# Attention and expert layer in one kernel: rows kept unnormalised, normalised after the gather, with queue and set-up in another order

## The chip, the cores and the metric

The kernel runs on one core of a Trainium2 chip. The core has a matrix engine (TensorE, PE; its weight loads are shown apart as PEld), a vector engine (VectorE, DVE), an activation engine (ScalarE, ACT), a general engine (GpSimd, POOL) and a queue that issues most DMAs (SyncE, SP). The metric is the device time of one launch in microseconds. Before the change it is 534.06 us, the median of 3 runs (533.18 to 534.73). One more execution was profiled: it took 532.09 us, with a span of 530.4 us.

## The reference

Causal attention over 4 batches of 12 heads with 448 positions and 64 columns a head, then one of 8 experts for each of the 1792 rows, all in float32.

```python
scores = np.where(causal, -1e9, (q @ k.T) / 8);  scores -= scores.max(-1)
attn = np.exp(scores);  attn /= attn.sum(-1) + 1e-9
x = (attn @ v).transpose(0, 2, 1, 3).reshape(1792, 768)
logits = x @ w_gate + modality_bias[modality_id]
e_idx = argmax(logits);  gate_w = softmax(logits)[e_idx]
for e in range(8):
    out[e_idx == e] = gate_w * (relu(x[e_idx == e] @ w1[e]) @ w2[e])     # 768 -> 1024 -> 768
```

## The kernel before, in words

**Precision.** Every large matmul is done in parts: an operand is split into a rounded high part and the rest (hi and lo), by a copy and a subtraction, and two or three products are added up in PSUM. The copies and subtractions are the main work of POOL and DVE.

**Attention.** The 48 heads are taken one per iteration, n = 0 to 47, as a software pipeline: iteration n computes the scores of head n (PE, L277), the row max of head n with the causal mask (DVE, L284), the exponentials of head n-1 (ACT, L294, which also gives the sums), the transposes of head n-2 (PE, L306) with their split (ACT L324, DVE L325), and the product with V of head n-3 (PE, L338, then ACT L363 and DVE L369). Four heads are a group (GH=4), three groups a batch. POOL splits q and k for two heads at a time (L185, L186, L189; tiles hl and kz), and SP stacks the parts by DMAs (L197, L198, tile st). POOL also splits V of a group into vh (L252, at n = 4k) and vl (L257, at n = 4k+1); PE's L338 needs both. `load_v` on SP brings the next group's V at n = 4k+2.

**Combining and normalising.** From n = 8 on, one block of 128 rows (64 for the first of a batch, four blocks a batch) of a finished group is combined per iteration: PE multiplies by a matrix wi that holds an identity and the gate weights, so that for each of the four heads 64 values of x and its 8 parts of the logits come out (L398, 288 columns). The softmax sums of the group have been inverted by then (L376, L383, tile rec). Even blocks are normalised by DVE from PSUM (`norm_l` L416, `norm_x` L426). Odd blocks are moved by ACT to SBUF (L408, tile cxt) and normalised by POOL with the same two lines. `norm_l` writes into ltp, where every head has a slot and one more slot holds the modality bias (POOL, L392, at the start of a batch; there are two such buffers). Finished rows of 768 columns are stored to xs in DRAM.

**Routing.** After each batch its logits are summed (L458), and one-hot marks (oh, L473), places by a matmul (L480) and gates (ent, L505) are computed by small operations, spread over the next iterations. POOL scatters the row numbers into four tables in DRAM (L509). After batch 1 the first expert is chosen and its weights loaded; `pre_ids` fetches slot numbers from the tables (idq, SP, L734) and `fetch_x` gathers rows (xg, POOL, L746) for the first expert block, so that its work begins between the last heads.

**The tail and the experts.** The section "tail" holds the last heads, the first expert products (`pre_g1`) and the last batch's routing, written out by hand. Then come steps, with counts that are known only at run time: each gathers 128 or 64 rows per place, transposes them (L755), multiplies by w1 (L765 to L767), applies relu, multiplies by w2 and scatters to out. At an expert's end w1 and w2 are replaced and split anew, by all of ACT, DVE (L685) and POOL (L681, L682).

**Order.** Instructions run in the order of the program on each engine; there is no scheduler. `iteration(n)` gives the order, with lists of later work: `later(n, f)` runs f behind the scores of iteration n, `soon` and `before` at other points. In set-up, ten small DVE operations make constants (L959 to L961 at n=0, L964 to L970 at n=1).

## Time and profile before

| | |
|---|---|
| median of 3 runs | 534.06 us (533.18 to 534.73) |
| profiled execution, its span | 532.09 us, 530.4 us |
| PE, PEld busy | 481.1 us (91%), 449.5 us (85%) |
| DVE, ACT, POOL busy | 319.2 us (60%), 273.7 us (52%), 290.5 us (55%) |
| granted PE clock, mean | 0.969 |
| largest groups | L294 on ACT 94.7 us, L765 to L767 on PE 68.0 us each, L325 on DVE 58.4 us, L189 on POOL 51.5 us |

The busy shares are means over two stages that differ: attention up to about 230 us, where every engine works, and the expert steps after it, where PE works nearly alone. A time is therefore read from the stretch that it belongs to. Positions in the text are microseconds from the start of the span. PE's clock is given as a share of its full 2.4 GHz.

### The profile page before, as it was taken

What the parts mean: (1) busy time and instruction counts of PE and PEld (TensorE: products, weight loads), DVE (VectorE), ACT (ScalarE), POOL (GpSimd) and SP (SyncE); (2) the same over time, 40 slices, a digit from 0 to 9 for tenths busy, and PEclk for the clock granted to TensorE, in tenths of its full rate; (3) what the DMA queues carried; (4) which work ended last, traced back from release to release, by engine and by line L of the source; (5) the groups of instructions that cost most, each with busy time, mean ns of one, the idle gap of its engine ahead of it and who ended that gap; (6) DMA issues with size and microseconds to landing.
All of it is one profiled execution on the core that took longest, in us unless ns stands there. A gap on an engine that the chain in (4) does not pass through costs nothing. (4 is left out here: it accounts for less than half of the span.)

```text
span 530.4 us, 10338 instructions
## 1 busy us (share of the span) xinstructions
PE 481.1 (91%) x3331; PEld 449.5 (85%) x3331; DVE 319.2 (60%) x882; ACT 273.7 (52%) x683; POOL 290.5 (55%) x303
## 2 busy tenths in 40 slices
PE   4598999999988979989899999999999999989971
PEld 4488889989968878878899999999999999978751
DVE  7988889999988979897521114552011110393690
ACT  4498899999977948724321124342111211551820
POOL 7799999989798797973220201752001001193581
PEclk9799999999989979999899999999999999999986
DMA  8687789987976398656369300973101001077000
GB/s 216 169 202 191 197 219 272 265 203 193 253 209 169 112 238 254 239 164 90 90 191 376 93 31 3 318 247 92 61 1 51 30 17 76 15 254 268 4 11 6
DMA packets 44137, 80.75 MB, mean 152 GB/s; under 512 B 15646, under 2 KB 27166, under 8 KB 44064
## 3 DMA queue, kind: packets, MB, share of 16 engines
q1 hardware_dynamic: 41024, 68.89, 46.2%
q0 software_dynamic: 3040, 11.03, 6.3%
q8 instruction: 28, 0.46, 0.4%
q14 instruction: 45, 0.37, 0.2%
HBM read 49.01 MB, written 11.89 MB: 115 GB/s over the span
## 5 line engine op out<-in xcount | busy, mean ns | idle before, releaser
L294 ACT ACTIVATE p<-p,nm 128x448 f32<-128x448 f32 x192 | 94.7, 497 | 9.5 <-DVE nm L284 9.5
L746 POOL DMA_INDIRECT xg<-xs,idg x18 | 20.3, 1126 | 139.1 <-DVEq L1327 75.2
L784 DVE SCALAR_TENSOR_TENSOR htl<-g,hth 128x256 fp32r<-128x256 f32 x40 | 16.7, 423 | 108.4 <-ACT hth L783 108.4
L765 PE MATMUL g<-xh,w1h 128*128 128x256 f32 x240 | 68.0, 283 | 0.0
L767 PE MATMUL g<-xh,w1l 128*128 128x256 f32 x240 | 67.9, 283 | 0.0
L766 PE MATMUL g<-xl,w1h 128*128 128x256 f32 x240 | 67.9, 283 | 0.0
L325 DVE TENSOR_TENSOR pl<-pt,ph 128x1024 fp32r<-128x1024 f32 x48 | 58.4, 1216 | 11.1 <-ACT ph L324 10.2
L306 PE MATMUL pt<-ident,p 128*128 128x128 f32 x432 | 64.8, 278 | 0.0
L338 PE MATMUL ot<-ph,vhl 128*128 128x448 f32 x192 | 50.8, 305 | 10.5 <-POOL vhl L257 6.4
L324 ACT ACTIVATE ph<-pt 128x1024 fp32r<-128x1024 f32 x48 | 48.9, 1019 | 13.1 <-PE pt L306 12.7
L189 POOL TENSOR_TENSOR kz<-raw,hl 64x448 fp32r<-64x448 f32 x44 | 51.5, 1170 | 6.9 <-DMA table<-ent,si 4.7
L306 PEld LDWEIGHTS pt<-ident,p 128*128 128x128 f32 x432 | 53.6, 150 | 0.6 <-issue 0.2
L783 ACT ACTIVATE hth<-g 128x256 fp32r<-128x256 f32 x40 | 15.2, 382 | 65.2 <-PE g L767 65.2
L277 PE MATMUL sa<-st 128*128 128x448 f32 x96 | 32.8, 342 | 17.2 <-DVE st L229 6.6
L825 POOL DMA_INDIRECT out_dram<-row,idg x14 | 15.0, 1074 | 56.9 <-ACTq L1311 32.2
L765 PEld LDWEIGHTS g<-xh,w1h 128*128 128x128 f32 x240 | 46.0, 192 | 0.2 <-DVE htl L784 0.2
L766 PEld LDWEIGHTS g<-xl,w1h 128*128 128x128 f32 x240 | 46.0, 192 | 0.0
L767 PEld LDWEIGHTS g<-xh,w1l 128*128 128x128 f32 x240 | 46.0, 192 | 0.0
L338 PEld LDWEIGHTS ot<-ph,vhl 128*128 128x128 f32 x192 | 33.8, 195 | 13.4 <-POOL vhl L257 7.4
L284 DVE CUSTOM_DVE_ANT_0 p<-sa,mask 128x448 f32<-128x448 f32 x96 | 36.3, 413 | 4.5 <-PE sa L277 3.8
L284 DVE CUSTOM_DVE_ANT_0 p<-sb,mask 128x192 f32<-128x192 f32 x96 | 36.3, 412 | 0.2
L294 ACT ACTIVATION_READ_ACCUMULATOR p<-p,nm 128x1 f32 x192 | 36.4, 189 | 0.0
(337 smaller groups left out, 1394.1 us busy)
## 6 DMA issues: line engine op xcount, KB each, us to landing
st<-hl SPq DMA_DIRECT2D x88, 224.0 KB
raw<-in_moe_w_dram SPq DMA_DIRECT2D x24, 512.0 KB
raw<-in_qk_dram SPq DMA_DIRECT2D x22, 448.0 KB
raw<-in_moe_w_dram SPq DMA_DIRECT2D x20, 384.0 KB
vraw<-in_v_dram SPq DMA_DIRECT2D x12, 384.0 KB
xs<-row SPq DMA_DIRECT2D x12, 384.0 KB
ut<-in_moe_w_dram SPq DMA_DIRECT2D x6, 384.0 KB
raw<-in_qk_dram SPq DMA_DIRECT2D x8, 224.0 KB
```

The costliest lines, as they stand in the source:

```text
L189: P.tensor_tensor(out=kz[m % 2][r, a], in0=x[r, 1], in1=hl[r, 2].bitcast(F32), op=ALU.subtract)
L277: nc.tensor.matmul(outs[i], lhsT=a[:, q0:q0 + n], rhs=z[:, :w], start=(last == 0), stop=(last == 1))
L284: V.tensor_tensor_reduce(out=z, in0=o, in1=m, scale=-scale, scalar=3.0e38, op0=ALU.add, op1=ALU.min, accum_out=nm[:n, i:i + 1],)
L294: A.activation(out=z, in_=z, func=AF.Exp, bias=nm[:n, i:i + 1], scale=-1.0, accum_out=sums[:n, b, i, h:h + 1],)
L306: nc.tensor.transpose(out=o, in_=a, identity=ident)
L324: A.activation(out=ph, in_=t, func=AF.Copy)
L325: V.tensor_tensor(out=pl, in0=t, in1=ph.bitcast(F32), op=ALU.subtract)
L338: nc.tensor.matmul(o[:, q0:S], lhsT=t[:rows, kt, h].rearrange("p a d -> p (a d)"), rhs=ph[:rows, c0:c1], start=(n == 0), stop=(n == 1),)
L746: P.indirect_dma_start(out=xg[u][:n], out_offset=None, in_=xs[0:rows, :], in_offset=bass.IndirectOffsetOnAxis(ap=g[:n, 0:1], axis=0), boun ...
L765: nc.tensor.matmul(o, lhsT=ah, rhs=bh, start=first, stop=False)
L766: nc.tensor.matmul(o, lhsT=ah, rhs=bl, start=False, stop=False)
L767: nc.tensor.matmul(o, lhsT=al, rhs=bh, start=False, stop=last)
```

## The change

1. **Combining.** All 288 columns of a block go into the row as they are: even blocks by one DVE copy from PSUM, odd ones by ACT (`take_x`). The row gets 12 more columns for reciprocal sums, so rows, xs and gathers have 876 columns. The order of columns in a row is now pairs of heads, 128 of x and 16 of logits.
2. **Sums.** One sum operation (POOL; DVE for the last batch) and four reciprocals per batch instead of three of each.
3. **Logits.** `norm_l` works from SBUF, once per block and batch, for all 12 heads (96 columns, DVE). For the last batch the first 8 heads are done before its gate work and the last 4 from PSUM.
4. **Gathered rows** are normalised in place by `norm_g`: the first block by DVE, every other by POOL, at the start of the step before (`norm_gs`).
5. **Bias.** One ltp buffer instead of two; the bias is added at the last group of the batch.
6. **POOL and SP order.** vh and vl are both made at n = 4k+1, behind the q/k split; `load_v` is issued at n = 4k, behind the stacking; the first expert's slot numbers are fetched two iterations later, rows of the first block two and one.
7. **Set-up.** The ten constants are made at n = 4 to 8; two of three subtractions for heads 2 and 3 move from n = 1 to n = 2, behind the max.

Numbers of lines are two to thirteen higher in the changed kernel (L284 becomes L286, L505 becomes L510).

**DVE at the start.** Before: the rows between the max of head 1 and the max of head 2; L964 to L970 are constants, L232 and L229 subtractions for heads 2 and 3.

```order
L232 TENSOR_TENSOR kz_150<-raw_113,st 64x448
L229 TENSOR_TENSOR st<-raw_114,st 64x448
L232 TENSOR_TENSOR kz_150<-raw_114,st 64x448
L964 TENSOR_SCALAR eq_98<-row 128x32
L965 CAST gt_99<-row 128x32
L966 SCALAR_TENSOR_TENSOR gt_99<-row,gt_99 128x32
L967 TENSOR_SCALAR ctri<-row 128x64
L968 TENSOR_SCALAR e_80<-evals 128x32
L969 TENSOR_SCALAR ebase<-evals 128x8
L970 TENSOR_SCALAR ebneg<-ebase 128x8
L284 ISA p_3_162,nm<-sa,mask 128x448
```

And the changed kernel, from the same place to the max of head 3:

```order
L234 TENSOR_TENSOR kz_147<-raw_113,st 64x448
L286 ISA p_3_159,nm<-sa,mask 128x448
L286 ISA p_0_156,nm<-sa,mask 64x64
L286 ISA p_1_157,nm<-sb,mask 128x192
L286 ISA p_2_158,nm<-sb,mask 128x320
L231 TENSOR_TENSOR st<-raw_114,st 64x448
L234 TENSOR_TENSOR kz_147<-raw_114,st 64x448
L327 TENSOR_TENSOR pl<-pt,ph 128x1024
L286 ISA p_3_151,nm<-sa,mask 128x448
```

The constants have left this place, and two subtractions stand behind the max of head 2 instead of ahead of it.

**SP around the slot numbers.** Before: idq are the slot numbers that are read from the tables, st the stacked parts of q and k for heads 42 and 43.

```order
L179 DMA raw<-in_qk_dram 128x896
L245 DMA vraw<-in_v_dram 128x3x256
L246 DMA vraw<-in_v_dram 64x256
L734 DMA idq<-table_70 128x2
L734 DMA idq<-table_71 128x2
L734 DMA idq<-table_72 128x2
L734 DMA idq<-table_73 128x2
L197 DMA st<-hl 64x896
L198 DMA st<-hl 64x2x448
```

And the changed kernel:

```order
L199 DMA st<-hl 64x896
L200 DMA st<-hl 64x2x448
L247 DMA vraw<-in_v_dram 128x3x256
L248 DMA vraw<-in_v_dram 64x256
L678 DMA raw_112<-in_moe_w_dram 128x1024
L181 DMA raw<-in_qk_dram 128x896
L738 DMA idq<-table_70 128x2
L738 DMA idq<-table_71 128x2
```

The stacking and the load of V now stand ahead of the fetches, and the next stacking behind them is that of heads 44 and 45.

**POOL at the end of attention.** Before: L392 is the bias add of the last batch, L509 the scatters to the tables, of which the first four belong to the batch before.

```order
L392 TENSOR_SCALAR ltp<-mb 128x4x8
L746 DMA xg_124<-xs,idg_1_118 128x768
...
L509 DMA table_70<-ent,si 14592x2
L509 DMA table_71<-ent,si 14592x2
L509 DMA table_72<-ent,si 14592x2
L509 DMA table_73<-ent,si 14592x2
L1224 TENSOR_TENSOR mask<-ident 128x64
L509 DMA table_70<-ent,si 14592x2
```

And the changed kernel, where L401 is the bias add and L438 the norm of a gathered block:

```order
L438 TENSOR_TENSOR xg_124<-xg_124 128x6x128
L686 TENSOR_SCALAR w1h_3171<-raw_114 128x1024
...
L514 DMA table_70<-ent,si 14592x2
L514 DMA table_71<-ent,si 14592x2
L514 DMA table_72<-ent,si 14592x2
L514 DMA table_73<-ent,si 14592x2
L1243 TENSOR_TENSOR mask<-ident 128x64
L401 TENSOR_SCALAR ltp<-mb 128x4x8
L514 DMA table_70<-ent,si 14592x2
```

The bias add, which the logits of the last batch wait for (L463 on DVE), moved behind four scatters and the mask.

```diff
+    XR = H * XW + H
...
-    lts = [ltp[:, j] for j in range(2)]
+    ltp = cst("ltp", [128, 512])
+    lt = ltp[:, 0:NTL * (H + 1) * E].rearrange("p (t h e) -> p t h e", t=NTL, h=H + 1)
...
-    def st_sums(gr, eng):
-        b, u = divmod(gr, NG)
-        r = sm([128, NTL, GH, 1], "rec")
-        eng.tensor_scalar(
-            out=r.rearrange("p t h o -> p t (h o)"), in0=sums[:, b, :, u * GH:(u + 1) * GH],
-            scalar1=1.0, scalar2=1e-9, op0=ALU.mult, op1=ALU.add,
-        )
-        rec[gr] = r
-
-    def st_rec(gr):
-        V.reciprocal(out=rec[gr], in_=rec[gr])
+    def pairs(x, lo, hi):
+        return x.rearrange("p (j c) -> p j c", c=2 * XW)[:, :, lo:hi].rearrange("p j (a d) -> p j a d", a=2)
+
+    def xcols(x):
+        return pairs(x[:, 0:H * XW], 0, 2 * D)
+
+    def lcols(x):
+        return pairs(x, 2 * D, 2 * XW)
+
+    def recs(x):
+        return x[:, H * XW:XR].rearrange("p (j a o) -> p j a o", a=2, o=1)
+
+    def st_sums(b, eng):
+        t = sums[:, b].rearrange("p t h -> p (t h)")
+        eng.tensor_scalar(out=t, in0=t, scalar1=1.0, scalar2=1e-9, op0=ALU.mult, op1=ALU.add)
+
+    def st_rec(b):
+        for i in range(NTL):
+            V.reciprocal(out=xrow[b, i][:, H * XW:XR], in_=sums[:, b, i])
 
     def st_comb(gr, i, x=None):
         b, u = divmod(gr, NG)
         q0, n = QT[i]
         if u == 0:
             xrow[b, i] = row()
-            if i == 0:
-                lt_all[b] = lts[b % 2]
-                P.tensor_scalar(
-                    out=lts[b % 2][:, :, H, :], in0=mb[:, b], scalar1=1.0, scalar2=0.0, op0=ALU.mult, op1=ALU.add
-                )
+        if u == NG - 1 and i == 0:
+            P.tensor_scalar(out=lt[:, :, H, :], in0=mb[:, b], scalar1=1.0, scalar2=0.0, op0=ALU.mult, op1=ALU.add)
         if x is None:
             x = bank("x")
         for j in range(GH // 2):
             nc.tensor.matmul(
                 x[:n, j * 2 * XW:(j + 1) * 2 * XW], lhsT=ots(gr, j)[:, q0:q0 + n],
-                rhs=wi[:, u * (GH // 2) + j].rearrange("p a c -> p (a c)"), start=True, stop=True,
+                rhs=wi[:, u * (GH // 2) + j], start=True, stop=True,
             )
-        cx[gr, i] = V, x
-
-    def st_move(gr, i):
+        cx[gr, i] = x
+
+    def take_x(gr, i):
+        b, u = divmod(gr, NG)
+        n = QT[i][1]
+        w = GH * XW
+        o, c = xrow[b, i][:n, u * w:(u + 1) * w], cx.pop((gr, i))[:n, 0:w]
         if i % 2:
-            c = cxt[:, (i // 2) * 384:(i // 2) * 384 + GH * XW]
-            n = QT[i][1]
-            A.activation(out=c[:n], in_=cx[gr, i][1][:n, :GH * XW], func=AF.Copy)
-            cx[gr, i] = P, c
-
-    def norm_l(gr, i):
+            A.activation(out=o, in_=c, func=AF.Copy)
+        else:
+            V.tensor_copy(o, c)
+
+    def norm_l(b, i, h0, h1, x=None):
+        n = QT[i][1]
+        c = xrow[b, i][:n, h0 * XW:h1 * XW] if x is None else x[:n, 0:GH * XW]
+        j = slice(h0 // 2, h1 // 2)
+        V.tensor_tensor(
+            out=lt[:n, i, h0:h1, :].rearrange("p (j a) e -> p j a e", a=2), in0=lcols(c),
+            in1=recs(xrow[b, i])[:n, j].to_broadcast([n, (h1 - h0) // 2, 2, E]), op=ALU.mult,
+        )
+
+    def st_norm(gr, i):
+        take_x(gr, i)
         b, u = divmod(gr, NG)
-        q0, n = QT[i]
-        eng, c = cx[gr, i]
-        xv = c[:n, :GH * XW].rearrange("p (h c) -> p h c", h=GH)
-        eng.tensor_tensor(
-            out=lt_all[b][:n, i, u * GH:(u + 1) * GH, :], in0=xv[:, :, D:XW],
-            in1=rec[gr][:n, i].to_broadcast([n, GH, E]), op=ALU.mult,
-        )
-
-    def norm_x(gr, i):
-        b, u = divmod(gr, NG)
-        q0, n = QT[i]
-        eng, c = cx.pop((gr, i))
-        xv = c[:n, :GH * XW].rearrange("p (h c) -> p h c", h=GH)
-        eng.tensor_tensor(
-            out=xrow[b, i][:n, u * GH * D:(u + 1) * GH * D].rearrange("p (h d) -> p h d", h=GH),
-            in0=xv[:, :, 0:D], in1=rec[gr][:n, i].to_broadcast([n, GH, D]), op=ALU.mult,
-        )
-
-    def st_norm(gr, i):
-        norm_l(gr, i)
-        norm_x(gr, i)
+        if u == NG - 1:
+            norm_l(b, i, 0, H)
+
+    def norm_g(u, n, eng):
+        x = xcols(xg[u])[:n]
+        eng.tensor_tensor(out=x, in0=x, in1=recs(xg[u])[:n].to_broadcast([n, H // 2, 2, D]), op=ALU.mult)
...
-        def setup_0():
-            V.tensor_copy(evals, itmp)
-            V.tensor_copy(tcol, ti)
-            V.tensor_copy(cth, cthi)
...
+        setup = [
+            (4, cast(tcol, ti)), (4, cast(evals, itmp)), (5, cast(cth, cthi)), (5, cast(gt64, tji)),
+            (6, cmp(eq1, dti, -1, ALU.is_equal)), (6, times_gt(gt64, dti, gt64)),
+            (7, cmp(ctri, ctri_i, 0, ALU.is_gt)), (7, fma(e8, evals, -1.0, float(E))),
+            (8, fma(ebase, evals[:, 0, :], float(NT), 0.0)), (8, fma(ebneg, ebase, 1.0, -float(EMPTY))),
+        ]
...
-        W1AT = (7, 9, 14, 14, 15, 15)
+        W1AT = (8, 9, 14, 14, 15, 15)
...
-                    later(n + 8 + t, lambda t=t: pre_ids(t))
-                    later(n + 11 + 2 * t, lambda t=t: fetch_x(0, 2 * S, t))
+                    later(n + 10 + t, lambda t=t: pre_ids(t))
+                    later(n + 13 + t, lambda t=t: fetch_x(0, 2 * S, t))
...
+            if n and n % GH == 0 and n < NHEAD:
+                load_v(n // GH)
...
-            if n == 1:
-                for f in subs:
+            if n in (1, 2):
+                for f in subs[:1] if n == 1 else subs[1:]:
...
+            if n == 0:
+                split_vh(0)
+                split_vl(0)
...
-            if n % GH == 1 and n > GH:
-                st_sums(n // GH - 1, P)
-            if n % GH == RECAT and n > GH:
-                st_rec(n // GH - 1)
-            if n % GH == 1 and n < NHEAD:
+            if n % (NG * GH) == 1 and n > 1:
+                st_sums(n // (NG * GH) - 1, P)
+            if n % (NG * GH) == RECAT and n > GH:
+                st_rec(n // (NG * GH) - 1)
+            if n % GH == 1 and n > 1:
+                split_vh(n // GH)
                 split_vl(n // GH)
...
-            if n % GH == 0 and n < NHEAD:
-                split_vh(n // GH)
...
-            if n % GH == 2 and n // GH + 1 < B * NG:
-                load_v(n // GH + 1)
...
+        def norm_gs(t):
+            if t < NSTEP:
+                for u in places_of(t):
+                    norm_g(u, BLK if t < SZ else HB, P)
...
+        norm_g(0, BLK, V)
         for half, p in enumerate((bank("sa"), bank("sb"))):
             x_trans(0, half, p, V)
...
+        norm_g(1, BLK, P)
         w1_chunk(3, P)
...
+        st_sums(B - 1, V)
+        st_rec(B - 1)
+        for i in range(NTL):
+            norm_l(B - 1, i, 0, H - GH)
...
-        st_sums(g, V)
-        st_rec(g)
         spare = two_banks()
         for i, bk in enumerate((bank("x"), bank("ot"), *spare)):
             st_comb(g, i, bk)
         for i in range(NTL):
-            norm_l(g, i)
+            norm_l(B - 1, i, H - GH, H, cx[g, i])
...
+        norm_gs(1)
         sd = schedule_b(*sc_)
         g2(ys, of_block(0), range(4, K2))
         y_out(0, 0, ys)
...
             ids_for(t + 2)
+            norm_gs(t + 1)
```

## Rows read from the trace of the kernel before

**Rows 1.** Windows: length; busy us (count) of PE, PEld, DVE, ACT, POOL; PE clock; DMA.

```profile
20.00:40.00 20.00, 16.59 (x116) 15.26 (x116) 17.66 (x52) 15.97 (x48) 15.55 (x21) 0.83 0.73 191
40.00:100.00 60.00, 56.97 (x459) 53.92 (x460) 52.27 (x171) 54.33 (x156) 56.32 (x76) 1.00 0.84 226
100.00:160.00 60.00, 56.50 (x444) 52.02 (x443) 54.54 (x178) 52.94 (x155) 53.70 (x59) 0.97 0.83 218
160.00:190.00 30.00, 24.07 (x187) 22.20 (x186) 26.35 (x83) 22.25 (x64) 23.85 (x26) 0.95 0.60 152
190.00:230.00 40.00, 38.30 (x280) 34.73 (x279) 37.64 (x97) 29.12 (x76) 35.73 (x34) 0.95 0.73 228
260.00:480.00 220.00, 218.46 (x1489) 213.75 (x1489) 66.47 (x122) 63.38 (x122) 54.75 (x38) 1.00 0.34 114
```

**Rows 2.** Timeline of PE, then DVE, 16 to 23 us: start, length, line

```profile
22.67 0.74 PE L277 MATMUL sa<-st 128*128 128x448 f32 x1 [6.09 <-DVE nm L284]
19.38 2.31 DVE L969 TENSOR_SCALAR ebase<-evals 128x8 f32<-128x8 f32 x1
```

**Rows 3.** Windows on stretches at half clock

```profile
22.67:26.69 4.02, 4.02 (x17) 3.74 (x18) 4.02 (x14) 2.82 (x9) 1.54 (x3) 0.50 0.40 114
156.40:159.80 3.40, 3.40 (x14) 2.53 (x14) 1.09 (x3) 2.25 (x8) 3.27 (x4) 0.50 0.75 208
188.75:193.90 5.15, 5.15 (x23) 4.99 (x24) 3.56 (x9) 0.56 (x1) 4.91 (x5) 0.50 0.85 224
255.40:258.80 3.40, 3.40 (x12) 3.40 (x12) 3.33 (x8) 0.00 (x0) 1.69 (x2) 0.50 0.56 136
```

**Rows 4.** Waits of PE, 30 to 160, then 160 to 260 us: total, times, longest

```profile
PE ot L338 <- POOL vhl L257: 6.4, 5, 2.2
PE sa L277 <- DMA st<-hl: 4.0, 1, 4.0
PE ot L766 <- DVE w2l L685: 2.0, 1, 2.0
PE x L480 <- DVE oh L474: 1.3, 1, 1.3
```

**Rows 5.** Timeline of SP, 176 to 184 us

```profile
176.93 7.46 SPq L734 DMA_DIRECT2D idq<-table  x4
```

**Rows 6.** Lines by form, POOL, then DVE: busy us, mean ns, idle before

```profile
L426 POOL TENSOR_TENSOR row<-cxt,rec 128x256 f32<-128x256 f32 x22 | 13.5, 614 | 0.0
L416 POOL TENSOR_TENSOR ltp<-cxt,rec 128x32 f32<-128x32 f32 x22 | 5.4, 244 | 3.8 <-ACT cxt L408 3.6
L682 POOL TENSOR_TENSOR w2l<-raw,w2h 128x768 fp32r<-128x768 f32 x3 | 6.7, 2230 | 0.2
L426 DVE TENSOR_TENSOR row<-x,rec 128x256 f32<-128x256 f32 x11 | 4.5, 406 | 0.0
L416 DVE TENSOR_TENSOR ltp<-x,rec 128x32 f32<-128x32 f32 x11 | 1.9, 173 | 0.0
```

**Rows 7.** Timeline of POOL, then DVE, 226 to 238 us

```profile
226.25 3.27 POOL L682 TENSOR_TENSOR w1l<-raw,w1h 128x1024 fp32r<-128x1024 f32 x1
232.03 1.49 POOL L509 DMA_INDIRECT table<-ent,si  x1 [1.75 <-DVE ent L505]
237.40 0.36 POOL L1224 TENSOR_TENSOR mask<-ident 128x64 f32<-128x64 f32 x1
227.16 2.40 DVE L494 TENSOR_TENSOR sl<-pc,oh 128x32 f32<-128x32 f32 x1
231.57 0.18 DVE L505 RECIPROCAL ent<-zs 128x4 f32<-128x4 f32 x1
233.66 0.96 DVE L458 TENSOR_REDUCE lg<-ltp 128x32 f32<-128x416 f32 x1
```

**Rows 8.** Timeline of PE, then POOL, 508 to 512 us

```profile
511.89 0.80 PE L840 MATMUL ot<-w2h,hth 128*128 128x512 f32 x1 [2.22 <-DVE hth L865]
508.28 2.40 POOL L682 TENSOR_TENSOR w2l<-wi,w2h 128x768 fp32r<-128x768 f32 x1
```

More of the change, by code (lines that the diff above doesn't have):

```diff
@@ L169, in attention_moe @@
     vraw = atp.tile([128, NTL, GH * D], F32, name="vraw")
-    raw, spl, vhl, sc, prob, pt, xrow, rec, lt_all, cx, rt, ov, ol = ({} for _ in range(13))
+    raw, spl, vhl, sc, prob, pt, xrow, cx, rt, ov, ol = ({} for _ in range(11))
     def ots(gr, j):
@@ L457, in logits @@
         def logits():
-            V.tensor_reduce(out=lg, in_=lt_all.pop(b).rearrange("p t h e -> p t e h"), axis=AX, op=ALU.add)
+            V.tensor_reduce(out=lg, in_=lt.rearrange("p t h e -> p t e h"), axis=AX, op=ALU.add)
         def top():
@@ L708, in open_moe @@
             w2l.append(moe.tile([128, DM], F32R, name=f"w2l{k}"))
-        raw2.extend(u.rearrange("p j s -> p (j s)")[:, 0:DM] for u in ut)
-        raw2.append(cxt)
-        raw2.append(wi.rearrange("p j a c -> p (j a c)")[:, 0:DM])
+        raw2.extend(big[:, j * DM:(j + 1) * DM] for j in range(3))
+        raw2.append(wi.rearrange("p j c -> p (j c)")[:, 0:DM])
         for k in range(len(raw2), K2):
@@ L754, in x_trans @@
             k = half * 3 + j
[L755 removed]
+            nc.tensor.transpose(out=p[:, j * 128:(j + 1) * 128], in_=xg[u][:, k * 2 * XW:k * 2 * XW + 128], identity=ident)
         o = p[:, 0:384].rearrange("p (k c) -> p k c", c=BLK)
@@ L833, in small_x @@
         for k in range(K1):
-            nc.tensor.transpose(out=o[:, k], in_=xg[u][:HB, k * 128:(k + 1) * 128], identity=ident[:HB, :HB])
+            nc.tensor.transpose(out=o[:, k], in_=xg[u][:HB, k * 2 * XW:k * 2 * XW + 128], identity=ident[:HB, :HB])
         A.activation(out=x[:, :, 0], in_=o, func=AF.Copy)
@@ L1065, in attention_moe @@
             later(NHEAD - KA + k, lambda k=k: w1_chunk(k, P))
-        later(0, setup_0)
-        later(1, setup_1)
+        for n, f in setup:
+            later(n, f)
         later(4, setup_4)
```

56 lines of the change are left out of this document (26 added, 30 removed).

## The prediction

> **What bounds the kernel now.** I read the stretches first [rows 1]: they show TensorE (PE) with hardly a hole from 260 to 480 us (218.46 us busy of 220). Nothing the change does to another engine can shorten that stretch; what it can win lies before 260, and what it can lose lies there or in the last steps. In the attention stage four engines run side by side at 85 to 95%: from 40 to 160 us PE is busy for 113.5 us, VectorE (DVE) for 106.8, ScalarE (ACT) for 107.3 and GpSimd (POOL) for 110.0 of 120. From 160 to 230 DVE is busy for 64.0 of 70 us. So a microsecond taken from POOL is won only as far as DVE or ACT were waiting for POOL, and what goes to DVE finds little free room.
>
> Second the waits of PE [rows 4]. Up to 160 us the entry is POOL's lower half of V (vhl, L257), five waits with 6.4 us. From 160 to 260 there is one wait of 4.0 us for the stacking DMAs of q and k (st<-hl), and 2.0 and 1.3 us on DVE in the routing of the last batch. At the start [rows 2] PE stands for 6.09 us before the scores that begin at 22.67: they wait for the max of the pass before (L284 on DVE), and DVE was in the set-up operations, of which one with 8 columns (L969) took 2.31 us.
>
> Third the granted clock [rows 3]. Behind four of the long holes TensorE runs at half clock (1.2 instead of 2.4 GHz): 4.02 us after the hole that ends at 22.67, 5.15 us after the one that ends at 188.75, 3.40 us from 156.40 and 3.40 us from 255.40. Work done at half clock would have taken half as long, so these cost 2.0, 2.6, 1.7 and 1.7 us beside the holes themselves.
>
> **The change part by part**, in microseconds won (+) or lost (-), against the profiled execution's 532.09.
>
> *Start to 80 us: +5.5 (from +1.5 to +10).* Seven set-up operations leave the place ahead of the third pass of L284, the last but one of which ended at 21.7 [rows 2], and three one pass earlier; they go, two at a time, into iterations 4 to 8. One of the three subtractions stays ahead of that pass and two go behind it, but head 3's scores wait for these. The hole of 6.09 should shrink by what the seven took, some 5.0 (2.31 of it L969), and a hole of about 1 us that is left should leave the clock up, since the 2.0 us of half clock came behind 6.09: +7.0. POOL loses the norms of odd blocks: 22 x (0.614 + 0.244) = 18.9 us in all [rows 6]. vl still stands behind the q/k split of its iteration, now with vh between, so it is not nearer by its place; but POOL has two norms less in every four iterations (1.7 us), and this adds up until it is ahead. Of the 6.4 us of vhl waits I count those before 80 us, some 3, as gone: +3. What is late next is DVE: the moved operations still cost their 5 us and more, each of them small, with SBUF operands alone, and L969 shows what such a one pays beside a busy POOL. In 40 to 100 us DVE has 7.7 us free of 60, so I give back 4.5. The low end is that the moved operations and POOL's set-up of this stretch eat all but the clock; the high end that only 1.5 or so is given back.
>
> *Norms of the logits on DVE, 80 to 160 us: -2 (0 to -5).* In batches 0 to 2 twelve tensor_tensor of 96 columns (norm_l) join DVE, with reciprocals 16 for 12. In return the even blocks are one copy of 288 columns instead of 0.406 + 0.173. By columns that copy is 0.46, which saves some 0.12 x 22 = 2.6 us. The trace has no norm_l: its nearest row from below is 0.173 for 32 columns from PSUM, from above L494 with two SBUF inputs, 2.40 us at 227.16, which ended when POOL's L682 (226.25 to 229.52) did [rows 7]. At 0.9 each, 10.8 us are added and 2.6 come off; they fall in four iterations of each batch, where DVE has no room, while batch 1's waits are partly covered. The odd blocks' norms were on POOL and off PE's path; that cover is gone.
>
> The row shows that a small operation with SBUF operands alone waits for the end of POOL's instruction (L494 beside L682), while L426 from PSUM took 0.406 throughout. The Trainium skill, "SBUF — State Buffer", section "SBUF: two separate sides", states that the port pair of DVE and GpSimd is an exclusive lock, taken for the whole instruction by a DVE operation with two SBUF inputs against a GpSimd one that reads SBUF. The trace agrees in this place. By that rule every norm_l and the norm of the gathered rows would wait so, and the terms on DVE stand at their far ends; without it at the near ones.
>
> *150 to 165 us: +3 (1 to 4).* The vhl wait of 2.2 us [rows 4] and the half clock behind it (1.7). With POOL lighter by 1.7 us in four iterations, and those since 80 us added up, both should go, less what DVE then limits.
>
> *165 to 217 us: +2.5 (-1 to +6).* SP issues in order. At 176.93 it took up the fetches of slot numbers (idq), which wait for the table scatters: 7.46 us [rows 5], and the stacking DMAs for head 42 stood behind them. The change puts the fetches two iterations later and behind the stacking: the 4.0 us wait and 2.6 us of clock go, 6.6 together. But DVE, at 64.0 of 70 us, gets a further four norm_l and the later idg reductions here, so I count well under half of it.
>
> *The tail to 230 us: -2.3 (-1 to -4.2).* The first gathered block is normalised on DVE ahead of its transposes, so PE, and everything queued on PE behind it (the last heads' PV and transposes), waits for it. By columns 3 x 0.41 = 1.2 us, plus between 0 and 3.27 for POOL, which splits w1 just then [rows 7]: I take 1.1. The second block is normalised on POOL, 2.23 us for 768 columns [rows 6], and its transposes come late enough.
>
> *The last batch's routing: -4.8 (-3 to -8.5).* This is the largest loss. The bias add that the logits need was done about 30 us earlier; with one buffer instead of two it now stands on POOL behind the four table scatters of the batch before. Those wait for that batch's gate (ent, ready at 231.75), start at 232.03, and with the mask behind them end at 237.76 [rows 7]; a small add (0.24) makes 238.0. The logits' reduction began at 233.66: 4.35 later. In front of ent now also stand one sum, four reciprocals and four norm_l (9 operations of some 0.2, 1.9 us): 6.2 together on a wait of PE that was 1.3 [rows 4]. A hole of 7.5 us costs the clock too; after the holes of 6.09 and 4.0 that was 2.0 and 2.6, say 2.3. Against it, PE is then so late that the 2.0 us wait for w2l and the 1.7 us of half clock behind it go: -6.2 - 2.3 + 3.7.
>
> *Expert steps: -1.5 (0 to -3).* POOL gets one or two norms of 2.23 us per step. Up to 480 us it is busy for 54.75 of 220, so they are hidden, and 14% more bytes in each gather as well. In the last small step POOL and DVE share the split of w2, PE waits 2.22 us for it and POOL's part has no slack [rows 8]; a norm ahead of it moves it by up to 2.2.
>
> *Sum:* 5.5 - 2 + 3 + 2.5 = +9.0 before 217 us, -2.3 - 4.8 - 1.5 = -8.6 behind it: +0.4, so 531.7 beside the 532.09 of the profiled execution. That one was 2.0 us quicker than the median of the runs, 534.06, so the forecast is 533.6, which is no change: 0.3%, what a measurement of this kernel can tell, is 1.6 us.
>
> **The rivals.** *The attention stage gives nearly all it can* (525.7): the start 9, norms -1, third term 4, queue 5, together +17, less the same 8.6. For it: every hole of PE before 217 us that [rows 2, 4] show has its releaser moved. Against it: DVE at 107 of 120 us takes the place of POOL.
>
> *DVE eats the gain, slower* (about 541): each norm_l, each set-up operation and the norm of the gathered block waits for a POOL instruction, as L494 and L969 did. Then the start is worth 3, norms -4, the third 2, the queue 0: +1, less a tail of 8.6: 541.7. It decides once a norm_l takes over about 1.2 us in the mean. For it: DVE's load; against it: POOL has 18.9 us less to hold the ports with. By the page's rule named above this is the outcome if POOL is nearly always in an instruction.
>
> *The bias add does not bind*: if ent comes several microseconds earlier against PE, since attention is no longer short of POOL, the tail costs 3 instead of 8.6 and the result is about 528. PE's order does not speak for it, as ent hangs on the same last heads.
>
> **How the numbers follow.** Balance as summed 0.45, with its own range 530 to 537; attention gives nearly all 0.25; bias add does not bind 0.08; DVE eats the gain 0.22. The balance alone splits as 0.15 faster, 0.18 within 1.6 us, 0.12 slower; so faster 0.48, same 0.18, slower 0.34. The range that holds 8 in 10 leaves out the outer parts of both rivals: 525 to 541.
>
> **What would show it.** PE's hole before the third scores under 2 us, and full clock there; no vhl and no st<-hl wait of over 1 us; norm_l near 0.9 us with a spread up to 2.4; a hole of 6 to 8 us ahead of the places of the last batch with the bias add as the last releaser; PE after it without the 2.0 us wait for w2l. If that hole is under 3 us the forecast is wrong by its largest loss; if PE's busy share in 160 to 217 us does not rise, by its queue term.

## The result, and the profile after

The changed kernel is slower: 536.76 us, the median of 10 runs (535.97 to 540.88), beside 532.89 for the kernel before (10 runs, 531.12 to 535.88). The ratio is 1.0088, 95% interval 1.0062 to 1.0113. A second series gave 1.0106 (1.0068 to 1.0145). The profiled execution took 536.24 us (span 534.5), 4.15 us more than that of the kernel before.

PE runs the same 3331 matmuls in the same order in both kernels, so the start of the same instruction can be compared. This gives the whole course of the loss:

| PE instruction | before, us | after, us | difference |
|---|---|---|---|
| third scores (L277, now L279) | 22.67 | 18.43 | -4.2 |
| product with V, head 12 (L338, now L340) | 73.89 | 69.29 | -4.6 |
| product with V, head 28 | 136.84 | 133.99 | -2.9 |
| scores of head 36 | 159.13 | 154.85 | -4.3 |
| scores and transposes behind the stacking wait | 192.25 | 183.51 | -8.7 |
| scores of head 47 | 212.11 | 206.64 | -5.5 |
| transposes of the first gathered block (L755, now L759) | 217.53 | 213.62 | -3.9 |
| places of the last batch (L480, now L485) | 236.52 | 237.64 | +1.1 |
| w1 products 6 us on | 243.18 | 246.90 | +3.7 |
| w2 products behind the w2l wait | 258.08 | 257.59 | -0.5 |
| the schedule's matmul behind the first block's w2 products (L651, now L656) | 260.98 | 261.46 | +0.5 |
| last small step, first w2 product (L840, now L844) | 511.89 | 514.41 | +2.5 |
| one of the last products of PE | 515.85 | 519.27 | +3.4 |

So attention does win, 5.5 us up to head 47; the tail takes this back to the last 0.5, which the last w2 product of the first block still has, and from the schedule's matmul on the expert steps lose 4 more. The last 0.5 us of the 4.15 lies behind PE's last matmul. The stretches of the changed kernel (length; busy time of PE, PEld, DVE, ACT, POOL; clock; DMA), to be read beside [rows 1]:

```profile
20.00:40.00 20.00, 17.62 (x127) 16.01 (x127) 18.04 (x58) 14.61 (x42) 18.49 (x28) 0.91 0.95 235
40.00:100.00 60.00, 59.45 (x481) 56.14 (x480) 56.12 (x174) 56.71 (x164) 51.31 (x54) 1.00 0.96 238
100.00:160.00 60.00, 55.61 (x451) 51.62 (x450) 55.27 (x173) 51.82 (x152) 45.55 (x41) 1.00 0.86 214
160.00:190.00 30.00, 25.59 (x194) 22.34 (x192) 29.32 (x87) 23.67 (x69) 25.47 (x24) 1.00 0.77 199
190.00:230.00 40.00, 35.97 (x256) 31.06 (x257) 36.94 (x102) 24.98 (x65) 29.42 (x19) 1.00 0.71 224
260.00:480.00 220.00, 217.62 (x1486) 212.90 (x1485) 67.41 (x127) 63.37 (x122) 70.20 (x51) 1.00 0.34 117
```

POOL is lighter by 5 to 8 us in each of the second and third rows, PE is fuller in the second (59.45 us for 56.97) but not in the third; DVE has become the fullest engine beside PE (55.27 of 60, then 29.32 of 30). From 260 to 480 POOL has 15 us more, the norms, and PE 0.8 less.

The waits of PE in the changed kernel (in total, times, longest), from 30 to 160, 160 to 262 and 262 to 525 us; [rows 4, 8] have those of before:

```profile
PE ot L340 <- POOL vhl L259: 5.7, 3, 2.8
...
PE x L485 <- DVE row L419: 6.6, 1, 6.6
PE ot L340 <- DVE big L371: 5.8, 7, 1.6
PE sa L759 <- DVE xg L438: 1.3, 1, 1.3
PE g L656 <- DVE ad L651: 0.9, 1, 0.9
...
PE ot L844 <- DVE hth L869: 3.6, 1, 3.6
PE ot L771 <- DVE htl L800: 0.9, 1, 0.9
```

The stacking wait (4.0) and the w2l wait (2.0) are gone. The vhl waits are not: 5.7 us for 6.4. In their place stand waits for DVE's output sum (L371), for the first gathered block's norm (L438) and 6.6 us ahead of the places. The profile names L419 there, a copy that DVE did later; what the matmul needs is the one-hot marks (L479), the end of a chain that starts with the logits. And 3.6 us stand ahead of the last w2 products, for 2.2 before.

How the logits came to be late: POOL's scatters and bias add, then the logits' reduction on DVE.

```profile
228.93 1.52 POOL L514 DMA_INDIRECT table<-ent,si  x1 [4.74 <-DVE ent L510]
234.60 0.24 POOL L401 TENSOR_SCALAR ltp<-mb 128x32 f32<-128x32 f32 x1
...
234.87 0.90 DVE L463 TENSOR_REDUCE lg<-ltp 128x32 f32<-128x416 f32 x1 [4.95 <-POOL ltp L401]
```

DVE stood for 4.95 us with all norms done, until POOL had issued four scatters, the mask and the bias add. That is the order that [rows 7] were read against, with every step of it as forecast: ent to scatters 0.3 us, scatters and mask 5.7, bias 0.24.

### The profile page after: what moved, and what is told of

The parts are those of the page before. It is cut to its first block, busy times and chain, and to the rows that moved or that the text cites. A ratio compares the mean times of both kernels' runs of the same rounds, so it can differ in the third digit from the quotient of the medians.

```text
span 534.5 us, 10254 instructions
## 1 busy us (share of the span) xinstructions
PE 482.2 (90%) x3331; PEld 446.8 (84%) x3331; DVE 325.6 (61%) x878; ACT 274.5 (51%) x685; POOL 294.8 (55%) x267
## 3 DMA queue, kind: packets, MB, share of 16 engines
q1 hardware_dynamic: 41024, 69.67, 47.2%
## 5 line engine op out<-in xcount | busy, mean ns | idle before, releaser
L340 PE MATMUL ot<-ph,vhl 128*128 128x448 f32 x192 | 50.0, 301 | 12.4 <-DVE big L371 6.5
L326 ACT ACTIVATE ph<-pt 128x1024 fp32r<-128x1024 f32 x48 | 48.9, 1019 | 7.6 <-PE pt L308 6.9
L340 PEld LDWEIGHTS ot<-ph,vhl 128*128 128x128 f32 x192 | 32.8, 190 | 16.1 <-POOL vhl L259 6.9
L829 POOL DMA_INDIRECT out_dram<-row,idg x14 | 14.6, 1041 | 53.7 <-ACTq L1330 32.0
L279 PE MATMUL sa<-st 128*128 128x448 f32 x96 | 32.6, 339 | 10.4 <-DVE st L231 8.3
L365 ACT ACTIVATE big<-ot 64x448 f32<-64x448 f32 x48 | 26.0, 541 | 23.6 <-PE ot L340 19.1
L286 DVE CUSTOM_DVE_ANT_0 p<-sa,mask 128x448 f32<-128x448 f32 x96 | 36.2, 412 | 1.3 <-PE sa L279 0.9
```

What stands on the lines that cost most here:

```text
L279: nc.tensor.matmul(outs[i], lhsT=a[:, q0:q0 + n], rhs=z[:, :w], start=(last == 0), stop=(last == 1))
L286: V.tensor_tensor_reduce(out=z, in0=o, in1=m, scale=-scale, scalar=3.0e38, op0=ALU.add, op1=ALU.min, accum_out=nm[:n, i:i + 1],)
L326: A.activation(out=ph, in_=t, func=AF.Copy)
L340: nc.tensor.matmul(o[:, q0:S], lhsT=t[:rows, kt, h].rearrange("p a d -> p (a d)"), rhs=ph[:rows, c0:c1], start=(n == 0), stop=(n == 1),)
L365: A.activation(out=t, in_=ov[g][64:128, :S], func=AF.Copy)
```

## The experiments

Ratios are to the kernel before, run on the same chip, with 95% intervals. Variants of the changed kernel are read beside its own 1.009 to 1.011.

**1. The bias add early.** Only the add's place is changed.

```diff
-        if u == NG - 1 and i == 0:
+        if u == NG - 1 and i == 0 and b < B - 1:
...
+        P.tensor_scalar(out=lt[:, :, H, :], in0=mb[:, B - 1], ...)   # ahead of the scatters
         norm_g(1, BLK, P)
```

> The changed kernel, with the bias add of the last batch alone moved ahead of the scatters on POOL (in front of the norm of the second gathered block). Theory: the hole of 6.55 us ahead of the last batch's places is the bias add behind the scatters. It shrinks to about 1.5 us, the half clock behind it goes, all of DVE's chain to the slot numbers moves forward by 5 us with it, and the 2.0 us wait for w2l near 255 us comes back: 3.5 us less than the changed kernel, about 533, ratio to before 1.000. Rival 1: the hole is hidden anyway by the chain of scatters and fetches that ends at 254 us; the hole goes and PE stands later instead, 0.5 us at most is won, ratio 1.008. Rival 2: the gate of the batch before is late, not the bias; the hole stays over 4 us.

Measured: 537.95 us, ratio 1.0122 (1.0079 to 1.0164). The theory fell and rival 1 holds. In this kernel's trace, POOL's last scatters, PE's waits, and the slot numbers' reduction on DVE:

```profile
241.89 0.97 POOL L514 DMA_INDIRECT table<-ent,si  x1 [1.18 <-issue]
246.20 0.97 POOL L514 DMA_INDIRECT table<-ent,si  x1 [3.34 <-DMA table<-ent,si]
...
PE ot L770 <- DVE w2l L690: 3.8, 1, 3.8
PE x L485 <- DVE row L419: 1.8, 1, 1.8
...
256.27 0.16 DVE L748 TENSOR_REDUCE idg<-idq 128x1 int32<-128x4 int32 x1 [5.91 <-DMA idq<-table]
```

The hole ahead of the places fell from 6.6 to 1.8 us, as expected. But the last batch's scatters, now issued earlier, wait for those of the batch before to land in the same tables (3.34 us at the fourth), the slot numbers come hardly sooner (46.5 us behind the scores of head 47, for 47.2 in the changed kernel), DVE waits 5.91 us for them with the w2 split behind, and PE waits 3.8 us for w2l. What sets the end of this stretch is the chain from the gate of batch 2 through eight scatters and the fetch to w2l. The hole lay beside it.

**2. No step norms.** `norm_gs` is left out, so rows of all but the first two blocks are not normalised.

```diff
-        norm_gs(1)
...
-            norm_gs(t + 1)
```

> The changed kernel without the POOL norms of the gathered rows in the steps (norm_gs); the rows of all blocks but the first two stay unnormalised. Theory: behind 258 us the changed kernel loses 0.97 us at 261 (a small DVE operation behind a norm on POOL), 0.8 at 483 and 1.2 + 0.9 at 514 us, as the norm stands ahead of POOL's share of the w2 split. All go: 3.6 us less than the changed kernel, ratio to before 1.001. Rival: the norms are hidden, and what was lost there comes from the wider rows and gathers; then under 1 us is won, ratio 1.007.

Measured: 534.11 us, 1.0026 (0.9998 to 1.0055): 0.6 to 0.8% less than the changed kernel, 3.3 to 4.3 us. The theory holds. PE's wait in the last small step is back to what it was:

```profile
PE ot L844 <- DVE hth L869: 2.2, 1, 2.2
```

In the changed kernel that wait comes about so (POOL, then PE):

```profile
508.44 1.49 POOL L438 TENSOR_TENSOR xg<-xg 64x768 f32<-64x768 f32 x1
510.80 2.40 POOL L687 TENSOR_TENSOR w2l<-wi,w2h 128x768 fp32r<-128x768 f32 x1
...
514.41 0.79 PE L844 MATMUL ot<-w2h,hth 128*128 128x512 f32 x1 [3.64 <-DVE hth L869]
```

The norm of the next block (1.49 us, whose result is wanted only later) stands ahead of POOL's w2 split, and DVE's part of that split took 2.56 us beside POOL's, where one of the same size took 0.96 in the tail; PE waits 1.4 us longer for it, and works at half clock for 5.3 us behind the wait, for 2.9 in the kernel before.

**3. No norm of any gathered row, with the bias late and early.** The first two blocks' norms are left out as well.

```diff
-        norm_g(0, BLK, V)
...
-        norm_g(1, BLK, P)
```

> The changed kernel without any norm of gathered rows (all gathered rows stay unnormalised), with the bias add where the change puts it. Beside the variant that also has the bias early (0.9984) it tells what the place of the bias add is worth. Theory: nothing, within 1 us: the hole of 6.5 us returns ahead of the places, and the wait for w2l (3.98 us at 252.7) goes, as PE is late; ratio 0.999. Rival: the hole costs its 5 us and its half clock; ratio 1.007.

> The changed kernel with the bias add ahead of the scatters and without any norm of gathered rows (the first two blocks on DVE and POOL and all steps; all gathered rows stay unnormalised). Theory: the steps give back 3.6 us as in the variant without the step norms, and the wait for the first block (1.3 us) goes; the chain that starts at the gate of the batch before (scatters, fetch, w2l) starts 1.5 us earlier, and with the bias early nothing else holds it: 5 to 6 us less than the changed kernel, ratio 0.998. Rival: the chain of scatters holds PE near 255 us whatever stands before it; then it gives only what the steps did, ratio 1.003.

Measured: 0.9991 (0.9964 to 1.0018) with the bias late, 0.9984 (0.9954 to 1.0015) with it early. PE's waits in the tail with the bias late, and then early:

```profile
PE x L485 <- DVE row L419: 5.7, 1, 5.7
```

```profile
PE ot L770 <- DVE w2l L690: 4.0, 1, 4.0
PE x L485 <- DVE row L419: 1.1, 1, 1.1
```

The same microseconds stand ahead of the places in the one and ahead of w2l in the other, and the times agree. Both theories hold in time; but with the bias early something still holds PE, 4.0 us for w2l, where the second theory said that nothing would. So the place of the bias add is worth nothing that can be told here, and the norms of gathered rows cost 1.0 to 1.2% of the time, 5 to 6 us: about 4 in the steps, the rest in the tail.

**4. Set-up and queue alone**, on the kernel before, which keeps its normalised rows: set-up; fetches (with the load of the first weights one iteration later, W1AT); both; and both again on another occasion.

```diff
-        later(0, setup_0)
-        later(1, setup_1)
+        for n, f in setup:                       # two each at n = 4 to 8
+            later(n, f)
...
-                for f in subs:
+                for f in subs[:1] if n == 1 else subs[1:]:
...
-                    later(n + 8 + t, lambda t=t: pre_ids(t))
+                    later(n + 10 + t, lambda t=t: pre_ids(t))
...
```

> The kernel before with the set-up and the two subtractions alone in their new places. Theory: the hole of 6.09 us falls to two of some 1.2, 4 us are won at 22 us, of which the q/k split and V on POOL give back about half by 60 us; 2 us less in all, ratio 0.996, and the rest of what set-up and queue won together (0.9915) is the queue's. Rival: the start carries all of it, ratio 0.992.

> The kernel before with the later fetches of slot numbers, rows and first weights alone. Theory: the wait of 4.0 us for the stacking at 188.7 us and its half clock go (6.6 us), DVE and vhl take most back by head 47: 1 to 2.5 us less than before, ratio 0.997. Rival: what set-up and queue gave together is the set-up's alone (0.9931 of 0.9915), and this is 1.000.

> The kernel before with two parts of the change alone: the set-up spread over n = 4 to 8 with two subtractions behind the max of head 2, and the fetch of slot numbers, rows and first weights later. Rows are normalised as before. Theory: the start gives about 4 us and the queue 2 to 3 at head 47, nothing is lost in the tail or the steps: 5 to 6 us less than before, ratio 0.990. Rival: what was won before 217 us came from POOL being freed of the odd norms; then POOL, as full as before, gives the start back in its vhl waits, and 2 us at most are won, ratio 0.997.

> The kernel before with set-up and fetches in their new places, once more: 0.9915 again, within 0.3%.

Measured: set-up 0.9931 (0.9901 to 0.9962), fetches 0.9958 (0.9924 to 0.9991), both 0.9915 (0.9885 to 0.9944) and again 0.9892 (0.9849 to 0.9934). Both parts pay, 3.7 and 2.2 us, and nearly add up. Set-up gave more than I expected of it, nearer to its rival (0.992), and the rival that POOL would take it all back is out: in the trace of set-up alone PE is 4.0 us ahead of the kernel before at head 47 and 3.6 at the end of the tail. Fetches alone are 0.3 us ahead at head 47; their gain stands in the tail, 2.8 us at its end.

**5. The order of V.** On the changed kernel the old order, on the kernel before with set-up and fetches the new one, and the old one on the changed kernel without norms of gathered rows.

```diff
-            if n % GH == 1 and n > 1:
-                split_vh(n // GH)
+            if n % GH == 1 and n < NHEAD:
                 split_vl(n // GH)
...
+            if n % GH == 0 and n < NHEAD:
+                split_vh(n // GH)
...
```

> The changed kernel with vh, vl and the load of V in their old order (vh at n = 4k, V loaded at n = 4k+2). Theory: in the changed kernel vh stands behind the q/k split, whose last subtraction waits for the landing of a scatter; the waits for vhl at 134 and 152 us (1.24 and 2.75) therefore shrink by about 1.05 each. The first one, at 38 us, moves by under 0.5. 1 to 2 us less at head 47, some 1 us less in all, ratio to before 1.006. Rival: the new order was what removed the waits at 58 and 74 us; they come back (1.2 and 0.6) and it is slower than the changed kernel by 1 to 2 us, ratio 1.011.

> The kernel before with set-up, fetches and also the new order of vh, vl and the load of V; rows are normalised as before. Theory: on a POOL that still has the odd norms, vh behind the q/k split makes vl later by 1.05 us where POOL is bound; a little slower than without it, ratio 0.994. Rival: the new order helps by itself (V's load and split of the first group earlier), ratio 0.989 or less.

> The changed kernel without any norm of gathered rows (they stay unnormalised) and with vh, vl and the load of V in their old order. Beside the one with the new order (0.9991) and the kernel before with set-up and fetches (0.9915). Theory: the new order of V is most of the 0.8% between these two, as it cost 0.5% on the kernel with normalised rows; ratio 0.994. Rival: the order of V costs nothing once POOL has no odd norms, and what is left is DVE's norm_l and the copies of 288 columns; ratio 0.999.

Measured: 1.0103 (1.0039 to 1.0167) for the changed kernel with the old order, no difference that can be told; 0.9968 (0.9935 to 1.0002) for the new order on the kernel before, where it costs 0.5% beside 0.9915; and 0.9989 (0.9956 to 1.0022) beside 0.9991. The theory holds where POOL still has the odd norms (the 0.5% is just clear of the noise of the two) and falls in time where it has not. There its first half is seen: with the old order on the changed kernel PE's vhl waits fall from 5.7 to 3.1 us and PE is 1.8 us earlier at 160 us; by head 47 it is 0.9 later. The wait that the theory speaks of is in the changed kernel's trace (POOL's row of work):

```profile
141.19 1.00 POOL L514 DMA_INDIRECT table<-ent,si  x1 [0.28 <-DMA st<-hl]
147.94 1.16 POOL L191 TENSOR_TENSOR kz<-raw,hl 64x448 fp32r<-64x448 f32 x1 [2.39 <-DMA table<-ent,si]
149.19 1.04 POOL L254 TENSOR_SCALAR vhl<-vraw 128x1024 fp32r<-128x1024 f32 x1
150.32 2.34 POOL L259 TENSOR_TENSOR vhl<-vraw,vhl 128x1024 fp32r<-128x1024 f32 x1
```

The second subtraction waits 2.39 us for the landing of the scatter issued at 141.19, and vh and vl, 3.4 us, stand behind it: the vhl wait of 2.8 us. POOL had time enough; it waited. The kernel before has the same wait, so its trace held it when the prediction was made (first row). The second row counts the waits that stand as instructions in POOL's queue at this line in the changed kernel:

```profile
143.68 1.16 POOL L189 TENSOR_TENSOR kz<-raw,hl 64x448 fp32r<-64x448 f32 x1 [1.62 <-DMA table<-ent,si]
...
L191 POOLq EVENT_SEMAPHORE  x6: 17/17/43, 121.0 to 178.6; - x6
```

From 100 to 215 us these waits of POOL for landed scatters come to 4.7 us before and 7.3 in the changed kernel.

**6. Where POOL's freedom went.** The last of these (0.9989) and the kernel with set-up and fetches alone (0.9892 in the same group) differ by what the change does to the combining, the sums, the bias and the width of a row. By the same instruction on PE the one with unnormalised rows is up to 7.7 us ahead at 165 us, level at 206, and 3.6 behind at the places. Its stretch from 160 to 210 us, and PE's waits from 160 to 212:

```profile
160.00:210.00 50.00, 41.48 (x308) 36.50 (x307) 47.35 (x137) 36.06 (x107) 39.32 (x33) 0.97 0.82 213
...
PE ot L340 <- DVE big L371: 6.3, 4, 3.0
PE sa L279 <- DVE nm L286: 2.1, 2, 1.9
```

And of the kernel with normalised rows:

```profile
160.00:210.00 50.00, 46.33 (x361) 43.38 (x360) 46.66 (x152) 41.25 (x119) 42.09 (x45) 0.96 0.79 209
...
PE ot L338 <- DVE ut L369: 1.8, 1, 1.8
PE ot L338 <- POOL vhl L257: 1.2, 1, 1.2
```

POOL has 2.8 us less to do there and waits of PE for it are gone; but PE stands 8.4 us for DVE's output sum and max instead of 1.8, and is emptier by 4.8. DVE is about as full in both (47.35 and 46.66 of 50). Read from this pair alone, what POOL's freedom won is lost where DVE is full. The other executions do not bear that out. The table gives, for the same matmuls of PE, how long four stretches took, in us (the first ends at the matmul that stands at 165.06 us in the kernel before):

| stretch | before | set-up and fetches, two executions | changed, two executions | without norms of gathered rows, new and old order of V |
|---|---|---|---|---|
| start to there | 165.1 | 165.3, 164.4 | 160.5, 163.5 | 164.5, 158.0 |
| to the scores of head 47 | 47.1 | 47.1, 42.4 | 46.2, 46.0 | 46.3, 48.9 |
| to the last w2 product of the first block | 48.4 | 46.5, 46.6 | 53.5, 53.7 | 50.6, 50.3 |
| to PE's last matmul | 258.2 | 259.8, 258.3 | 262.3, 262.5 | 257.9, 258.7 |

The pair above holds the shortest and the longest time of the second stretch, and set-up and fetches took 42.4 us in one execution of their kernel and 47.1 in the other. So a loss on DVE is not shown there, and the next run does not show it either. At head 47 the changed kernel stands at 206.6 and 209.5 us, set-up and fetches alone at 212.4 and 206.8: a gain or loss of the attention stage by the freed POOL is within what one kernel's two executions differ by. What repeats is the tail (third stretch). Without norms of gathered rows it takes 49.8 to 50.6 us in three kernels with unnormalised combining. With normalised rows and the fetches moved it takes 45.9 to 48.1 in five executions, and 51.5 in one, with the new order of V, where the clock fell in its first part. So combining makes it 2 to 4 us longer; the norms of the first two blocks add 3, and the steps' norms about 4 behind it. Without norms the hole ahead of the places is 5.7 and 5.3 us, for 0.4 and 1.7; but with the bias early and that hole at 1.1 the tail still takes 49.8 us, so the hole's removal alone does not give them back. What in the combining lengthens the tail is open.

**7. norm_l of odd blocks on POOL**, in batches 0 to 2.

```diff
-        V.tensor_tensor(
+        (P if i % 2 and b < B - 1 else V).tensor_tensor(
```

> The changed kernel with norm_l of odd blocks on POOL instead of DVE in batches 0 to 2. Theory: DVE saves six operations of 0.3 to 1.6 us in iterations that it limits, POOL has room for them: the waits for the output sum (L371) between 165 and 208 us, 4 us together, shrink by 1 us in all; ratio 1.008 against 1.010. Rival: norm_l holds nothing, and the change is within noise of 1.010; it is slower if POOL's vhl gets later by them.

Measured: 542.48 us, 1.0151 (1.0101 to 1.0202), from six runs in two groups: 536.9 and 537.7 us, which is the changed kernel's own time, and four from 542.4 to 543.2. The theory fell: nothing is won, and the waits for L371 are 5.6 us for 5.8. The profiled execution is one of the four; of its 6.3 us 1.6 are lost up to the end of the tail and 4.7 behind it (2.0 us before the schedule's matmul, for 0.9, half clock behind it, and 1.7 behind PE's last matmul), not where the edit is. Why is open.

**8. Batch 0's scatters behind the split**, with set-up and fetches moved, rows normalised; run twice.

```diff
-                later(n + 7 + (2 * i, i // 2, 0)[b], lambda i=i: scatter([i]))
+                if b == 0:
+                    soon(n + 8 + 2 * i, lambda i=i: scatter([i]))
...
```

> The kernel before with set-up and fetches in their new places (0.9915), and the four scatters of batch 0 behind the q/k split and vl of the next iteration instead of ahead of them. Theory: the last subtraction of a q/k split waits for the landing of the scatter issued 4 us before, and vl behind it is what PE waits for at 136 and 155 us (0.8 and 2.3 us); the next split is then two iterations off, and both waits go: 2 us less, ratio 0.988. Rival: POOL is bound by its own work there, and nothing is won; or the scatters of batch 1 wait for these later ones and 1 us is lost.

> The kernel before with set-up, fetches and batch 0's scatters behind the split, once more, beside the one with the scatters in their old place in the same group. Theory: 0.984 to 0.988 against 0.991; the scatters are worth 2 to 4 us. Rival: the two differ by chance of the clock behind holes and agree here within 0.3%.

Measured: 523.81 us, 0.9843 (0.9799 to 0.9887), and 525.79 us, 0.9870 (0.9829 to 0.9911), beside 0.9915 and 0.9892 without it. This is the fastest version here, and beats both kernels. Whether the scatters' place adds to set-up and fetches is not settled: it was ahead both times, by 0.7 and 0.2%, and the second lies within the interval. POOL's waits for landed scatters from 100 to 200 us only fell from 4.7 to 4.0 us, and PE's waits for vhl from 30 to 212 us did not fall (7.0 and 5.4 us in the two executions, for 5.5 and 4.7), so the mechanism expected is not what the time shows.

**9. The changed kernel again.**

> The changed kernel once more, unchanged, beside the others of this group. Theory: its ratio to before is what it was, 1.009 (1.006 to 1.012), and the variants of it are to be read against this run. Rival: on this chip it stands at 1.012 or more, and the bias add moved forward, at 1.012, was then no loss.

Measured: 537.95 us, 1.0106 (1.0068 to 1.0145); the ratio 1.0122 with the bias early is not told apart from it. Its profiled execution (539.41 us) was 2.8 us later at head 47 than the first one, and for 2 us of it the reason shows. The 3.4 us behind the vhl wait near 153 us, in the first profile of the changed kernel:

```profile
152.71:156.11 3.40, 3.40 (x24) 2.93 (x25) 2.43 (x6) 2.10 (x8) 3.24 (x4) 1.00 0.56 129
```

And the same place in the second:

```profile
154.23:157.63 3.40, 3.40 (x13) 2.57 (x14) 1.35 (x3) 1.36 (x5) 3.24 (x4) 0.54 0.57 134
```

The holes were 2.75 and 3.09 us long. After the one the clock stayed up and PE ran 24 matmuls in 3.40 us; after the other it fell to half and it ran 13.

## Why the prediction was wrong

The prediction said no change, with 0.48 for faster; it is slower by 0.9%, a case that it gave 0.34. The time lies in the range, the direction was not forecast. By its own terms, with what the profiled executions show:

| term | forecast | measured |
|---|---|---|
| start to 80 us | +5.5 | +4.6 |
| norm_l on DVE, to 150 us | -2 | -1.3 |
| 150 to 165 us, vhl and its clock | +3 | +1.3 |
| 165 to 217 us, queue | +2.5 | +0.8 |
| first gathered block | -2.3 | -1.5 |
| routing of the last batch | -4.8 | -3.4 |
| expert steps | -1.5 | -4 |
| sum | +0.4 | -3.5 |

The largest miss is the last term: the prediction's step "so they are hidden" failed, as the norms in the steps cost 4 us in place of 1.5. The next two are 150 to 165 us and the queue, each 1.7 us short.

**Start.** The hole was right: 6.09 us became two of 1.66 and 1.00. The step "should leave the clock up" was not: the clock stayed up through both holes and fell behind them, for 3.41 us in this execution.

```profile
21.40:24.81 3.41, 3.25 (x14) 2.72 (x14) 3.39 (x14) 2.33 (x9) 3.18 (x4) 0.50 0.99 257
```

In the second execution of the same kernel it was 1.00 in this window, and PE was 1.2 us earlier at 26 us; but it then stood 2.36 us for vhl at 38 us, for 1.70, and the two executions are level there (38.13 and 38.25). So the clock of the start was worth next to nothing by 38 us. The runs with set-up alone put the start at 3.7 us net.

**150 to 165 us.** The step that failed here is "this adds up until it is ahead": POOL was ahead, but a wait on its queue that the sum did not hold, for the landing of a scatter, kept vhl late, and the change had put vh (1.04) behind that wait. The wait stood in the trace of the kernel before (1.62 us at 143.68). Only the half clock went, and the second profile shows that not even that is certain.

**165 to 217 us.** The stacking wait and its clock went as said: at 192 us PE was 8.7 us ahead, 4.1 more than at 165, of the 6.6 us. Of these 3.3 were gone by head 47, where PE waits for DVE's output sum (L371) and max. The forecast "well under half" was still too much, by 1.7 us, and in another execution of set-up and fetches alone this stretch is as long as before (47.1 us), so its size is not certain to a few us. norm_l came out near what I took: 4.8 us for nine blocks and 2.9 for three, 7.7 beside 10.8. The copy of 288 columns took 0.44 for 0.46:

```profile
L419 DVE COPY row<-x 128x288 f32<-128x288 f32 x11 | 4.8, 439 | 0.0
L425 DVE TENSOR_TENSOR ltp<-row 128x96 f32<-128x96 f32 x9 | 4.8, 532 | 0.3
L425 DVE TENSOR_TENSOR ltp<-row 64x96 f32<-64x96 f32 x3 | 2.9, 977 | 0.1
```

The mean of 0.53 us for the nine, with 0.26 to 1.65 for one, shows the waiting that L494 had shown, but mostly short. By the rule of the Trainium skill ("SBUF — State Buffer", "SBUF: two separate sides") each could have waited for a whole POOL instruction. The trace agrees for the longest ones only. And where the first gathered block was normalised, DVE took 0.94 us while POOL's w1 split, which had begun 0.4 us before, took 3.60 instead of 2.39: there it was POOL that gave way.

**The routing.** Each step of the order was right (a hole of 6.6 for the 7.5 forecast, half clock behind it, the w2l wait gone), and what they add up to was read wrongly. I counted the hole as a loss with something given back; the runs with the bias early show that it costs nothing, as the chain through scatters and fetch ends at the same time without it. From the gate of batch 2 (ent) to the end of the w2l wait or, where there is none, of that split, it took 23.4 us before, 26.4 in the changed kernel and still 25.5 with the bias early, as the scatters then wait for one another. The gate itself comes 22.0 us behind the scores of head 47, for 19.6 before; without the norms of gathered rows it is 19.4. So the norms of the first two blocks put off the gate too, and cost the tail 3 us in all, not the 1.5 that the table gives to the first block.

**The expert steps.** This is the term that turned the sign: the runs without norms give 3.3 to 4.3 us for the steps alone where 1.5 (0 to 3) was forecast. The last small step was named, at 1.5 us, and took 1.2 and another 1.1 at half clock; the two places missed, 0.9 and 0.8 us, are 261 us, where a small DVE operation took 1.31 beside a norm, and 483 us, the change of expert before the last one. One pass of the norm is 1.48 us, not 2.23: the price was too high and the number of places too low.

**The rivals.** Slower by DVE alone (0.22) came nearest of them in time but not in mechanism: its price for norm_l was not reached, and the larger part of the loss is in norms of gathered rows. "The bias add does not bind" asked for an earlier gate, which did not come; that the place of the add costs nothing is true for another reason, and it was not worth the 528 us: the chain behind it held.

In all: set-up and fetches win 0.85 to 1.1%, the norms of gathered rows lose 1.0 to 1.2%, and the unnormalised combining, which should have been the gain, loses some 0.8 to 1.0% more, of which the traces place 2 to 4 us in the tail (experiment 6); the cause there is open.

## What to carry to other kernels

A hole on the busiest engine is a loss only if nothing else ends at the same place later: before pricing it, follow the next wait behind it back to its start, and see whether that chain passes through the hole. Work moved from a shared stage into a loop that "has room" must be priced at each place where the loop's own critical part runs on the same engine, here the schedule and the last two changes of expert; from 262 to 480 us the norms cost nothing. And an engine that is lightened gains only if what others waited for was its own work; part of POOL's lateness was waits for landings. Last, one execution of each of two kernels is too little to place a loss of a few microseconds: the same stretch of one kernel took 42.4 and 47.1 us.

## What was not expected of the hardware

The granted clock behind the same place of one program is not the same in each execution, and the length of the hole alone does not decide it: after 2.75 us the clock stayed at 1.00, after 3.09 us it was 0.54, and after 1.70 us at 38 us in one profile 1.00 while the other, after 2.36, had 0.54. By the windows shown, a fall costs about 1.6 us here (3.4 us at 0.54), an estimate, and runs of one kernel differ by 4 to 8 us.

The second subtraction of a q/k split waited for a scatter in flight that does not touch its tiles (2.39 us). The EVENT_SEMAPHORE row shows the wait as an instruction of POOL's queue at this line, and in the trace it names the scatter's own semaphore; so the wait is the program's and no stall of the chip that these runs would show. Why the program has it was not tried.
